# Key-value sums on full-height tiles, values split around a query pass, output transposes behind one wait

## The chip, the cores and the metric

The kernel runs on one core of one Trainium2 chip. The metric is device time in microseconds (us), taken as the median of several executions. A profile is one further execution, recorded by the hardware profiler. TensorE, the matrix engine, is called PE, its weight loads PEld; VectorE is DVE, ScalarE is ACT, GpSimd is POOL, and SP is the engine that issues most DMAs.

## What is computed

Input x has 2048 rows of 448. It is normalised row by row (xn), and two branches are added to it: linear attention with 16 heads of width 28 and a learned feature map, and a feed-forward branch of width 1792.

```python
q, k, v = split_heads(xn @ wqkv)                 # 16 heads, Dh = 28
pq, pk  = q @ w_phi, k @ w_phi                   # per head
phi_q = concat(softmax(pq), softmax(-pq))        # 56 features
phi_k = concat(softmax(pk), softmax(-pk))
kv  = einsum("sf,sd->fd", phi_k, v);  z = phi_k.sum(s)     # per head, over all rows
o   = (phi_q @ kv) / (phi_q @ z + 1e-6)
out = x + concat_heads(o) @ wo + silu(xn @ w1) @ w2
```

The sums kv and z run over all rows, so no query row can be finished before the last key row is in.

## The kernel before

**Tiles.** The rows are worked on as 8 pairs (`NPAIR`) of two tiles of 128 rows (t = 0, 1). All contractions over the 448 features are written for half-height tiles: `mms` issues two matmuls of 64 rows each, one on partitions 0 to 63 (`UP`) and one on 64 to 127 (`LO`), into two banks of PSUM, and PE works on both at once. `contract` makes two passes of this, the second with the halves exchanged; the second pass adds into the banks that the other half wrote, so each of its steps waits (`syncs`) for the last step of the first pass to be complete. With four k-steps in the first pass and three in the second, a pass over 448 columns is 8 or 6 matmuls.

**Stages.** First normalisation and transposes of xn, the folding of w_phi into the key and query weights, and the first layer of the feed-forward branch for pairs 0 to 5 (`ffn1_chunk`). Then the projection stage, one round for each pair p: keys (`k_macro`, name pk_mm, banks 0 and 1), values (v_mm, banks 2 and 3), one group of queries (`q_group`, pq_mm, banks 6 and 7, 512 columns). ACT takes exp of keys (twice 128x896 elements) and of queries (twice 128x1024). DVE copies the values to SBUF (v_ev), sums the keys' exponentials (Sk), takes reciprocals (Rk), and POOL multiplies (phik); for pair 7 this is done tile by tile, with the second tile's phik on DVE. `k_acc(p)` then adds pair p into the sums: for each of 2 tiles, 2 signs and 4 groups of heads one step of four matmuls, 64 rows by 64 columns with 58 columns streamed, two of them into bank 4 (rows 0 to 63) and two into bank 5 (rows 64 to 127). DVE joins the two banks into KVZ under a mask (kvA, then kvz twice). In the last stage, for each pair, `q_products` (U_mm) multiplies queries by KVZ into banks 2 to 5, `q_divide` normalises on DVE (L888 to L901) and adds the two signs on POOL in five pieces (oadd, L920), `o_transpose` turns the result with 14 transposes on PE into banks 6 and 7, from where ACT writes oT (oT_ev), and `out_pair` accumulates 14 matmuls of w2 and 4 of wo for each tile in banks 0 and 1; DVE adds x and SP stores.

**Order.** Nothing is issued in the order in which it is written down. `P.op` records an operation with an estimated duration, its data dependences (`deps`, turned into semaphore waits between engines) and order-only dependences (`odeps`, same engine). `schedule` then makes a static list schedule with these estimates, and each engine runs its list in order. A `prio` of 0 goes before 1 and 2: the feed-forward layer for pairs 6 and 7 has prio 1 and the output tiles prio 2, so they fill PE where the rest is expected to wait. A change of tile shape on PE (`table`) is charged 98 ns in this plan. The projection stage is the exception: its PE order is written out as a chain of order-only dependences,

```python
chain += [k12[0], v12[0], k12[1], v12[1], q12[0], kv, q12[1]]     # L841, kv = k_acc(p - 2)
chain += [k_acc(NPAIR - 2), k_acc(NPAIR - 1)]                     # L842, after the loop
```

with index 0 and 1 for first and second pass. So the key-value sums of pair p - 2 lie between the first and the second query pass of pair p, and for p = 0 and 1 nothing lies there. Prio 1 work can lie between entries of the chain.

**Buffers.** Ek (exponentials of the keys) and vaug (values with a column of ones) have 3 slots (NEK) in one tensor `scr`, first all Ek, then all vaug. `wraw` holds raw query and key weights early and the float32 output of q_divide (`o_both`) late.

## Time and profile before

| what | value |
|---|---|
| median of 3 runs | 165.26 us (164.93 to 165.86) |
| the profiled execution, time and span | 165.84 us, span 164.1 us |
| PE busy | 158.3 us, 96% of the span |
| DVE, ACT, POOL busy | 102.3, 73.8, 54.5 us |
| granted PE clock | 1.00 throughout |
| key-value matmuls, 64x64 tiles, 58 columns (L444) | 512, from 58.2 to 89.6 us |
| output transposes (L457, from 103 us on) | 112, from 103.3 to 140.0 us |

The span is the time from the first to the last instruction of the program in the profile; the execution's own time is 1.74 us longer. Rows of groups give busy time and the mean of one instruction, but matmuls are pipelined: what one costs is read from the distance of starts in the timeline, where a row is a run of like instructions (start, duration with the modelled end of the last, count). The chain of waits is the work that ended last, followed back from the end of the run.

### The profile page before, as it was taken

The page shows a single profiled execution, that of the slowest core. Times are in us where ns is not written, and L with a number is a line of the kernel's source. Part 1 is how long each engine was busy: PE and PEld are TensorE (multiplying, and loading weights), DVE is VectorE, ACT ScalarE, POOL GpSimd, SP SyncE. Part 2 cuts the span into 40 slices and gives each one's busy share as a digit, 9 for nine tenths or more (in the row PEclk, how much of TensorE's full clock was granted, in tenths as well). Part 3 has the DMA queues.
Part 4 walks back from the last instruction along what each step waited for, and adds up shares of the span by engine and source line. Part 5 has one row for each costly group of instructions (what it writes and reads, how often), then busy time and mean ns, then how long its engine had stood idle before and what let it go on. Part 6 is the DMA issues. An engine that isn't in the chain of part 4 may idle for free.

```text
span 164.1 us, 5978 instructions
## 1 busy us (share of the span) xinstructions
PE 158.3 (96%) x2741; PEld 102.7 (63%) x2741; DVE 102.3 (62%) x185; ACT 73.8 (45%) x85; POOL 54.5 (33%) x79
## 2 busy tenths in 40 slices
PE   6999999999999999999999999999999999999994
PEld 4689799999754455545557865555555554455563
DVE  2859878932418887666878788578867865111211
ACT  3542756569688866786667562210220131200000
POOL 7021130110001777755574052553464265000000
PEclk9999999999999999999999999999999999999999
DMA  5974743000003332120000000010101010101011
GB/s 162 311 202 116 203 129 108 0 4 4 4 0 112 116 112 60 46 72 4 4 4 6 0 4 4 0 56 4 50 10 56 0 60 2 56 3 56 0 62 50
DMA packets 8197, 9.24 MB, mean 56 GB/s; under 512 B 1324, under 2 KB 7916, under 8 KB 8172
## 3 DMA queue, kind: packets, MB, share of 16 engines
q1 hardware_dynamic: 7868, 8.62, 17.1%
q8 instruction: 21, 0.34, 0.8%
q10 hardware_dynamic: 304, 0.25, 0.5%
q14 instruction: 4, 0.03, 0.1%
HBM read 7.02 MB, written 1.84 MB: 54 GB/s over the span
## 4 chain that ended last, share of the span: by engine, by line
PE 83%; DVE 7%; DMA 3%; ACT 2%; SPq 2%; issue 1%; DVEq 0%; ACTq 0%
PE psum L444 47%; PE psum L438 33%; PE psum L457 3%; DMA w_sb<-in_B_w_dram 3%; DVE scr L798 2%; SPq L536 2%; DVE wraw L901 1%; DVE Sk L795 1%; ACT oT L463 1%; ACT scr L463 1%; DVE den L892 1%; DVE KVZ L854 1%; DVE kvt L849 0%; DVE R L888 0%; DVE rden L895 0%
## 5 line engine op out<-in xcount | busy, mean ns | idle before, releaser
L444 PE MATMUL psum<-xnT,w_sb 64*128 64x256 bf16 (+1 forms) x938 | 49.4, 252 | 1.0 <-DMA w_sb<-in_B_w_dram 0.6
L438 PE MATMUL psum<-w_sb,hT 128*128 128x448 bf16 (+2 forms) x238 | 47.1, 342 | 0.0
L444 PEld LDWEIGHTS psum<-xnT,w_sb 64*128 64x128 bf16 x938 | 39.2, 94 | 5.4 <-PE psum L444 1.1
L463 ACT ACTIVATE hT<-psum 128x1024 bf16<-128x1024 f32 (+2 forms) x29 | 28.5, 995 | 21.7 <-PE psum L444 21.7
L438 PEld LDWEIGHTS psum<-w_sb,hT 128*128 128x128 bf16 x238 | 22.0, 98 | 18.9 <-issue 0.4
L798 POOL TENSOR_TENSOR scr<-scr,Rk 128x1792 bf16<-128x1792 bf16 (+1 forms) x8 | 24.2, 3021 | 22.8 <-DVE Rk L797 15.3
L920 POOL TENSOR_TENSOR xn_sb<-wraw 128x8 bf16<-128x8 f32 (+4 forms) x40 | 21.3, 564 | 30.1 <-DVE wraw L901 23.8
L941 DVE TENSOR_TENSOR out_sb<-psum,x_sb 128x448 bf16<-128x448 f32 (+2 forms) x17 | 10.1, 595 | 22.1 <-PE psum L438 22.1
L463 ACT ACTIVATE oT<-psum 128x896 bf16<-128x896 bf16 x8 | 7.3, 917 | 33.8 <-PE psum L457 28.3
L463 ACT ACTIVATE EqT<-psum 128x1024 bf16<-128x1024 f32 x16 | 15.5, 1021 | 8.4 <-PE psum L444 8.4
L901 DVE TENSOR_TENSOR wraw<-psum,Gq 128x1792 f32<-128x1792 f32 (+1 forms) x9 | 16.3, 1814 | 1.0 <-DVE Gq L896 0.5
L795 DVE TENSOR_REDUCE Sk<-scr 128x64 f32<-128x1792 bf16 (+1 forms) x9 | 16.2, 1811 | 1.1 <-ACT scr L463 0.5
L467 DVE CAST scr<-psum 128x896 bf16<-128x896 f32 x8 | 8.8, 1094 | 11.7 <-PE psum L444 11.7
L438 PE MATMUL psum<-wo_sb,oT 128*128 128x448 bf16 (+2 forms) x68 | 14.9, 342 | 0.1
L444 PE MATMUL psum<-xnT,wqk_sb 64*128 64x512 bf16 x112 | 14.8, 378 | 0.1
L463 ACT ACTIVATE scr<-psum 128x896 bf16<-128x896 f32 x16 | 13.8, 914 | 1.0
L599 POOL TENSOR_TENSOR rstd<-ve,neghalf 128x2 f32<-128x2 f32 (+1 forms) x8 | 5.3, 660 | 24.2 <-DVE ve L598 24.2
L444 PE MATMUL psum<-wqk_sb,xnT 64*128 64x448 bf16 x112 | 13.2, 349 | 0.0
L444 PE MATMUL psum<-wv_sb,xnT 64*128 64x448 bf16 x112 | 13.2, 349 | 0.0
L590 DVE BATCH_NORM_STATS2 st<-x_sb 128x6 f32<-128x448 bf16 x16 | 9.7, 613 | 3.6 <-DMA x_sb<-in_A_x_dram 3.6
L438 PEld LDWEIGHTS psum<-wo_sb,oT 128*128 128x128 bf16 x68 | 6.4, 98 | 5.9 <-ACT oT L463 0.5
L444 PEld LDWEIGHTS psum<-wqk_sb,xnT 64*128 64x128 bf16 x112 | 5.4, 94 | 5.4 <-ACT scr L463 0.2
(54 smaller groups left out, 120.1 us busy)
## 6 DMA issues: line engine op xcount, KB each, us to landing
out_dram<-out_sb SPq DMA_DIRECT2D x7, 224.0 KB, 2.0
w_sb<-in_B_w_dram SPq DMA_DIRECT2D x3, 448.0 KB, 3.3
x_sb<-in_A_x_dram SPq DMA_DIRECT2D x2, 448.0 KB, 3.4
w_sb<-in_B_w_dram SPq DMA_DIRECT2D x2, 384.0 KB, 4.7
x_sb<-in_A_x_dram SPq DMA_DIRECT2D x3, 224.0 KB, 5.7
wraw<-in_A_wqkv_dram SPq DMA_DIRECT2D x1, 672.0 KB, 4.3
w_sb<-in_B_w_dram SPq DMA_DIRECT2D x1, 576.0 KB, 6.4
wv_sb<-in_A_wqkv_dram SPq DMA_DIRECT2D x1, 336.0 KB, 4.0
```

The lines of the kernel that those rows point to most:

```text
L438: lambda e: e.matmul(dst, lhsT, rhs, start=start, stop=stop, skip_group_check=True),
L444: r = e.matmul(dst, lhsT, rhs, start=start, stop=stop, skip_group_check=True)
L457: out = e.transpose(dst, src, ident[r, 64:128] if r == LO else ident[r, 0:64])
L463: return P.op("act", d_act(_cols(src)), lambda e: e.activation(dst, src, func, scale=scale), reads=[src], writes=[dst], table=table, name= ...
L467: return P.op("dve", dur, lambda e: e.tensor_copy(dst, src), reads=[src], writes=[dst], name=name)
L590: P.op("dve", 600, lambda e: e.bn_stats(st6[:, t, :], x_sb[:, t, :]), reads=[x_sb[:, t, :]], writes=[st6[:, t, :]], name="bnst")
L599: P.op("pool", 580, lambda e: e.tensor_tensor(r2, v2, nh, ALU.pow), reads=[v2, nh], writes=[r2], name="rstd")
L795: P.op("dve", d_dve(896 * n), lambda e, S4=S4, E4=E4: e.tensor_reduce(S4, E4, AXL.X, ALU.add), reads=[E4], writes=[S3], name="Sk")
L798: P.op("dve" if t0 else "pool", d_dve(896) if t0 else d_pool(896 * n, 1.57), lambda e, E4=E4, R4=R4, n=n: e.tensor_tensor(E4, E4, R4[:, :, ...
L901: P.op("dve", d_dve(896 * n), lambda e, dsto=dsto, U=U, G3=G3, n=n: e.tensor_tensor(dsto, U[:, :, :, 0:DH], G3[:, :, :, None].broadcast_to ...
L920: P.op("pool", d_pool(_cols(dst), 2.26), lambda e, dst=dst, a0=a0, a1=a1: e.tensor_tensor(dst, a0, a1, ALU.add), reads=[a0, a1], writes=[d ...
L941: P.op("dve", d_dve(c1 - c0), lambda e: e.tensor_tensor(dst, ob, xs, ALU.add), reads=[ob, xs], writes=[dst], name="out_ev")
```

## The change

It does five things. (1) `k_acc` takes whole 128-row operands: a step is two matmuls of 128 rows by 64 columns instead of four of 64 by 64, and all go to bank 4; kvA and the two kvz become one operation from bank 4 to KVZ. (2) The sums of two pairs lie together between the query passes of p = 3, 5 and 7 (pairs p - 3 and p - 2), where before one pair lay there for p = 2 to 7; a fourth slot for Ek and vaug is taken from wraw, and the slots are laid out one by one. (3) For p = 0, 1, 2, 4, 6, of the three steps of the second value pass the last lies between the two query passes. (4) All sums of pairs 6 and 7 depend on the last phik, and lie together. (5) Every output transpose of a pair depends on the last oadd of that pair. The planned duration of a key-value step goes from 33 to 27 ns.

```diff
@@ -368,18 +368,19 @@
         BD = sb("BD", [128, 5, 56], BF16)
         hT = sb("hT", [128, FT, 2, NPAIR, 128], BF16)
         EqT = sb("EqT", [128, 4, 2, 2, NPAIR * 128], BF16)
-        NEK = 3
+        NEK = 4
+        SLOT = 2 * (EW + H * DV)
         wraw = sb("wraw", [128, 4, 2 * D + 64], BF16)
         o_both = wraw[:].rearrange("p k c -> p (k c)")[:, 0:8 * D].bitcast(F32).rearrange("p (q c) -> p q c", q=4)
-        scr = sb("scr", [128, NEK * 2 * (EW + H * DV)], BF16)
+        scr = sb("scr", [128, 3 * SLOT], BF16)
         wT = scr[:, 0:9 * 512].rearrange("p (a c) -> p a c", a=9)
-        Ek = scr[:, 0:NEK * 2 * EW].rearrange("p (b t c) -> p b t c", b=NEK, t=2)
-        vaug = scr[:, NEK * 2 * EW:NEK * 2 * (EW + H * DV)].rearrange("p (b t h d) -> p b t h d", b=NEK, t=2, h=H)
+        slots = [scr[:, i * SLOT:(i + 1) * SLOT] for i in range(3)] + [wraw[:].rearrange("p k c -> p (k c)")[:, 0:SLOT]]
+        Ek = [a[:, 0:2 * EW].rearrange("p (t c) -> p t c", t=2) for a in slots]
+        vaug = [a[:, 2 * EW:SLOT].rearrange("p (t h d) -> p t h d", t=2, h=H) for a in slots]
         NOB = 3
         o_sum = xn_sb
         oT = sb("oT", [128, NOB, 7, 128], BF16)
         KVZ = sb("KVZ", [128, 2, 4, 2, DZ], BF16)
-        kvt = sb("kvt", [128, 8, 2, DV], F32)
         ident = sb("ident", [128, 128], BF16)
         ones_bf = sb("ones_bf", [128, 128], BF16)
         ones4 = sb("ones4", [128, 4], F32)
@@ -783,13 +784,13 @@
             k12 = proj(p, lambda r, k: wqk_sb[r, k, 1, :, 0:56], 0, "pk_mm")
             kb = psum[:, 0:1024].rearrange("p (t c) -> p t c", t=2)[:, :, 0:D]
             for s in range(2):
-                exp_act(Ek[:, sl, :, s * D:(s + 1) * D], kb, 1.0 if s == 0 else -1.0, "exp_k")
+                exp_act(Ek[sl][:, :, s * D:(s + 1) * D], kb, 1.0 if s == 0 else -1.0, "exp_k")
             v12 = proj(p, lambda r, k: wv_sb[r, k, :], 2, "v_mm")
             vb = psum[:, 1024:2048].rearrange("p (t c) -> p t c", t=2)[:, :, 0:D].rearrange("p t (h d) -> p t h d", h=H)
-            copy_dve(vaug[:, sl, :, :, 0:DH], vb, "v_ev", d_dve(896))
+            copy_dve(vaug[sl][:, :, :, 0:DH], vb, "v_ev", d_dve(896))
             for t0, t1 in ((0, 2),) if p < NPAIR - 1 else ((0, 1), (1, 2)):
                 n = t1 - t0
-                E4 = Ek[:, sl, t0:t1, 0:2 * D].rearrange("p t (h f) -> p t h f", f=DH)
+                E4 = Ek[sl][:, t0:t1, 0:2 * D].rearrange("p t (h f) -> p t h f", f=DH)
                 S3, R3 = Sk[:, sl, 32 * t0:32 * t1], Rk[:, sl, 32 * t0:32 * t1]
                 S4, R4 = (a.rearrange("p (t h) -> p t h", t=n) for a in (S3, R3))
                 P.op("dve", d_dve(896 * n), lambda e, S4=S4, E4=E4: e.tensor_reduce(S4, E4, AXL.X, ALU.add),
@@ -808,14 +809,13 @@
                 for s in range(2):
                     for c in range(4):
                         parts = []
-                        for i, r in enumerate((UP, LO)):
-                            for j in range(2):
-                                hp = 2 * c + j
-                                parts.append((banks[4 + i][64 * j:64 * j + 64, (4 * s + c) * 58:(4 * s + c + 1) * 58],
-                                              Ek[r, sl, t, s * D + hp * 56:s * D + hp * 56 + 64],
-                                              vaug[r, sl, t, 2 * hp:2 * hp + 2, :].rearrange("p h c -> p (h c)"),
-                                              first and s == 0 and c == 0, last))
-                        ops.append(mms(parts, "kv_mm", 33.0, 32))
+                        for j in range(2):
+                            hp = 2 * c + j
+                            parts.append((banks[4][64 * j:64 * j + 64, (4 * s + c) * 58:(4 * s + c + 1) * 58],
+                                          Ek[sl][:, t, s * D + hp * 56:s * D + hp * 56 + 64],
+                                          vaug[sl][:, t, 2 * hp:2 * hp + 2, :].rearrange("p h c -> p (h c)"),
+                                          first and s == 0 and c == 0, last))
+                        ops.append(mms(parts, "kv_mm", 27.0, 32))
             return ops
 
         def q_group(ch, c):
@@ -828,32 +828,34 @@
             return done
 
         for sl in range(NEK):
-            P.op("pool", d_pool(32), lambda e, sl=sl: e.memset(vaug[:, sl, :, :, DH], 1.0),
-                 writes=[vaug[:, sl, :, :, DH]], name="vaug1")
-            P.op("pool", d_pool(16), lambda e, sl=sl: e.memset(Ek[:, sl, :, 2 * D:EW], 0.0),
-                 writes=[Ek[:, sl, :, 2 * D:EW]], name="ekpad")
+            P.op("pool", d_pool(32), lambda e, sl=sl: e.memset(vaug[sl][:, :, :, DH], 1.0),
+                 writes=[vaug[sl][:, :, :, DH]], name="vaug1")
+            P.op("pool", d_pool(16), lambda e, sl=sl: e.memset(Ek[sl][:, :, 2 * D:EW], 0.0),
+                 writes=[Ek[sl][:, :, 2 * D:EW]], name="ekpad")
         P.cur_prio = 0
         chain = []
         for p in range(NPAIR):
             k12, v12 = k_macro(p)
-            kv = k_acc(p - 2) if p > 1 else []
             q12 = q_group(p // 4, p % 4)
-            chain += [k12[0], v12[0], k12[1], v12[1], q12[0], kv, q12[1]]
-        chain += [k_acc(NPAIR - 2), k_acc(NPAIR - 1)]
+            if p > 1 and p % 2:
+                chain += [k12[0], v12[0], k12[1], v12[1], q12[0], k_acc(p - 3), k_acc(p - 2), q12[1]]
+            else:
+                chain += [k12[0], v12[0], k12[1], v12[1][:2], q12[0], v12[1][2:], q12[1]]
+        kv = k_acc(NPAIR - 2) + k_acc(NPAIR - 1)
+        ready = [o.id for o in P.ops if o.name == "phik"][-1]
+        for o in kv:
+            o.deps.add(ready)
+        chain.append(kv)
         chain = [c for c in chain if c]
         for a, c in zip(chain, chain[1:]):
             for o in c:
                 o.odeps.add(a[-1].id)
 
-        bA, bB = (banks[4 + i][:, 0:464].rearrange("p (a h d) -> p a h d", a=8, h=2) for i in range(2))
+        bA = banks[4][:, 0:464].rearrange("p (a h d) -> p a h d", a=8, h=2)
+        dkv = KVZ[:].rearrange("p s c h d -> p (s c) h d")[:, :, :, 0:DV]
         P.op("dve", d_dve(464), lambda e: e.tensor_tensor(
-            kvt[:], bA, mask2[:, None, :, None].broadcast_to([128, 8, 2, DV]), ALU.mult),
-            reads=[bA, mask2[:]], writes=[kvt[:]], name="kvA")
-        for hl in range(2):
-            src, tt, dst = bB[:, :, hl, :], kvt[:, :, hl, :], KVZ[:].rearrange("p s c h d -> p (s c) h d")[:, :, hl, 0:DV]
-            P.op("dve", d_dve(232), lambda e, src=src, tt=tt, dst=dst, hl=hl: e.scalar_tensor_tensor(
-                dst, src, mask2[:, hl:hl + 1], tt, ALU.mult, ALU.add),
-                reads=[src, mask2[:, hl:hl + 1], tt], writes=[dst], name="kvz")
+            dkv, bA, mask2[:, None, :, None].broadcast_to([128, 8, 2, DV]), ALU.mult),
+            reads=[bA, mask2[:]], writes=[dkv], name="kvz")
 
         UB = 2
         U4 = psum[:, UB * 512:UB * 512 + 2048].rearrange("p (q c) -> p q c", q=4)[:, :, 0:480].rearrange("p q (h c) -> p q h c", c=DZ)
@@ -873,6 +875,8 @@
                                           EqT[r, c, s, t, p * 128:(p + 1) * 128],
                                           KVZ[r, s, c, :, :].rearrange("p h d -> p (h d)"), True, True))
                         mms(parts, "U_mm", 31.0)
+
+        oadd_last = {}
 
         def q_divide(p):
             q = p % 2
@@ -920,11 +924,14 @@
                 P.op("pool", d_pool(_cols(dst), 2.26), lambda e, dst=dst, a0=a0, a1=a1: e.tensor_tensor(dst, a0, a1, ALU.add),
                      reads=[a0, a1], writes=[dst], name="oadd")
 
+            oadd_last[p] = P.ops[-1].id
+
         def o_transpose(p):
             ob = o_sum[:, p % NOB, :]
             for j in range(7):
                 trs([(bank16[6 + h][:, 64 * j:64 * j + 64], ob[r, 128 * j:128 * j + 128], r)
                      for h, r in enumerate((UP, LO))], "oT_tr")
+                P.ops[-1].deps.add(oadd_last[p])
             src = psum16[:, 6 * 1024:8 * 1024].rearrange("p (b c) -> p b c", b=2)[:, :, 0:448].rearrange(
                 "p b (j u) -> p b j u", u=64)
             act(oT[:, p % NOB, :, :].rearrange("p j (b u) -> p b j u", b=2), src, ACTF.Identity, "oT_ev")
```

## The prediction

> **What bounds it now.** I read the busy shares first (PE 96% at full granted clock), then the chain of waits by line and in order of time, then PE's timeline stage by stage. The chain as a whole:
>
> ```profile
> PE 83%; DVE 7%; DMA 3%; ACT 2%; SPq 2%; issue 1%; DVEq 0%; ACTq 0%
> ```
>
> PE's own work sets the end, with one interruption of note. In the chain in order of time (start, duration, what) it is this:
>
> ```profile
> 53.98 28.33 PE psum L444 x558
> 82.31 0.02 issue
> 82.33 1.73 ACT scr L463 x2
> 84.07 0.02 issue
> 84.09 2.08 DVE Sk L795 x2
> 86.17 0.48 DVE Rk L797 x2
> 86.65 0.02 issue
> 86.67 2.64 DVE scr L798
> 89.32 0.04 issue
> 89.36 0.66 PE psum L444 x32
> 90.02 0.02 issue
> 90.05 0.65 DVE kvt L849
> 90.70 0.02 issue
> 90.72 0.84 DVE KVZ L854 x2
> ```
>
> Up to 82.3 us every nanosecond that PE is spared is earned. From there the last pair's exponentials, their sums and the second tile's phik (86.67 to 89.31) lead to KVZ at 91.56 and, over the DVE steps of L888 to L901, to the query product at 97.80; PE fills that time with feed-forward matmuls. Behind it PE is packed again to the end: from 140.43 us every output matmul takes 189 ns.
>
> PE's timeline of the projection stage (start, duration, group; duration includes a modelled tail, so I go by starts):
>
> ```profile
> 52.89 1.92 PE L444 MATMUL psum<-xnT,wqk_sb 64*128 64x512 bf16 x14
> 54.64 0.92 PE L444 MATMUL psum<-wqk_sb,xnT 64*128 64x448 bf16 x8
> ...
> 62.37 1.03 PE L444 MATMUL psum<-xnT,wqk_sb 64*128 64x512 bf16 x8
> 63.33 0.89 PE L444 MATMUL psum<-scr 64*64 64x58 bf16 x64
> 64.14 0.82 PE L444 MATMUL psum<-xnT,wqk_sb 64*128 64x512 bf16 x6
> ```
>
> and the output transposes of the last two pairs:
>
> ```profile
> 134.14 0.29 PE L457 MATMUL psum<-ident,xn_sb 64*128 64x64 bf16 x8 [0.23 <-ACT oT L463]
> 134.36 0.36 PE L438 MATMUL psum<-w_sb,hT 128*128 128x448 bf16 x1
> 134.66 0.26 PE L457 MATMUL psum<-ident,xn_sb 64*128 64x64 bf16 x6
> ...
> 138.74 0.26 PE L457 MATMUL psum<-ident,xn_sb 64*128 64x64 bf16 x6
> 138.94 0.36 PE L438 MATMUL psum<-w_sb,hT 128*128 128x448 bf16 x1
> 139.23 0.20 PE L457 MATMUL psum<-ident,xn_sb 64*128 64x64 bf16 x2
> ```
>
> **The empty gap (p = 0, 1).** Both query passes stand in one row of 14 matmuls, 52.89 to 54.64 = 1.75 us; seven steps at 0.216 us (the spacing within a pass) are 1.51. So 0.24 us are lost to the second pass's wait. The value step put there takes 0.19 us (448 columns: 0.76 us for eight matmuls) and is taken out elsewhere. Gain 0.19 x 2 = **0.38 us**, 0.05 of wait staying.
>
> **One visit of key-value sums now.** A round with one lasts 59.72 to 64.80 = 5.08 us; a round without lasts 50.24 to 54.64 = 4.40, less the 0.24 of wait 4.16. So a visit costs 0.92 us: 64 matmuls and two changes of tile shape of about 0.09 each. The visit of p = 7 costs only 0.73 (64 matmuls from 83.65 to 84.29). Single starts in the trace tell why: a step of four stands 31.7 ns behind the one before as long as PE has instructions in hand; in the rounds p = 2 to 6 this ends after ten steps, and then a step takes 59 ns, 14.8 for each matmul and its load. PE is being fed too slowly.
>
> **One visit after.** No row shows a tile of 128 rows by 64 columns. Half the instructions per step: feeding allows 2 x 14.8 = 29.5 ns. From the array's side the nearest rows are pairs of half-height matmuls of like length (transposes, 64 columns: 27.2 ns a pair; U_mm, 60 columns: 28.4) and the present step of 31.7. I take 29 ns, ends 27 and 31.7. Shape changes: U_mm and transposes between output matmuls pay 0.11 going in and 0.12 going out, so 0.21 a visit. 32 steps: 0.93 + 0.21 = **1.14 us** for two pairs.
>
> Up to pair 7's key pass (80.05 us): before 5 x 0.92 = 4.60; after 2 x 1.14 (p = 3, 5) + 3 x 0.05 (waits left at p = 2, 4, 6) = 2.43. Saved 2.17, with the 0.38 above **2.55 us**.
>
> **What the moved step delays.** In even rounds the values are complete 0.86 + 0.19 us later, 3.5 us into the round; v_ev (1.09) then ends at 4.80, and the next value pass over banks 2 and 3 begins at 4.97: covered, by 0.17 less a semaphore's delay. Behind v_ev on DVE stand Sk and Rk; round 6's Rk then ends 3.3 us into round 7, and v_ev(7) and Sk(7) start 0.44 us later than now. Exps of keys end 4.0 us into a round of 4.2, so banks 0 and 1 are free in time. phik, which POOL ends well over 2 us ahead of its visit, loses no cover. The w2 and wo loads hang on exps of even rounds and start sooner. Two more memsets on POOL (0.11 and 0.16 us each) lie in its 11.5 us of idle time before 52.8.
>
> **From round 7 to KVZ.** Work: round 7's visit 1.14 for 0.73 (+0.41); the last two pairs now cost 0.73 + 0.74 without waiting, after 1.14 (-0.33). Together +0.08. The chain: +0.44 (above); behind the last phik stand 32 steps of 29 ns (0.93) instead of 8 (0.25), +0.68; one KVZ operation of 0.64 for 0.65 + 0.84 and a gap, -0.87. So +0.25. Waiting: PE now loses 0.48 between the tiles of pair 7 (64 matmuls take 0.99 us from first to last start, not 0.51), 0.13 before the first U_mm and 0.54 before 97.80. The new wait on the last phik stands in front of 32 steps, and behind it in PE's list lie U_mm and all fillers. The plan gives that phik 1.08 us (`d_dve(896)`), the trace 2.63, so PE should arrive early by over 1 us where it now loses 0.48: I take +0.6 us of waiting. Ends: all three waits gone but for the longer chain (-0.9), and +1.2. Sum of this part **-0.7 us**.
>
> **Transposes in one go.** An interruption costs a change in and out, 0.23 us: (134.66 - 134.36 = 0.30, less 0.19 for the matmul = 0.11) plus 0.12. Pair 6 has one too many, pair 7 two: **+0.69 us**. Their wait for oadd's last piece costs nothing while w2 matmuls lie ahead of them, as they do; without that cover PE would stand up to 2.7 us (five oadd pieces). The wait of 0.4 us for oT before 134.14 might go as well; end +0.4. Pairs 0 to 5 already go 14 at a time.
>
> **Sum.** 2.55 - 0.7 + 0.7 = 2.55 us. The profiled execution's span of 164.1 becomes 161.55, its time of 165.84 would be 163.3; it lies 0.58 above the median. From the median of 165.26: **162.7 us**.
>
> **Rivals.** *(a) Weights are not loaded under running matmuls on full-height tiles: slower.* Today a step has tiles of two row halves, and one half can load while the other runs; afterwards both tiles fill all rows. For it: the two steps at the start of a visit, where no weights lie ready, stand 52 ns apart (83.65 to 83.70), and a 64x64 load takes 107 ns by its row. Against it: 128x128 output matmuls of 128 columns, each with new weights, stand 55.9 ns apart, which leaves no room for a load. Price: load 52 + matmul 29 = 81 ns, 52 more for 4 x 32 steps = 6.7 us: 169.4. It decides from a step of about 56 ns on. The Trainium skill, "TensorE: Matmul & The Clock Gate", Part 3 (The mechanism), says that weight loads overlap running matmuls only where the row group differs, which speaks for this; the 55.9 ns row disagrees. *(b) Loads bind only partly,* a step of about 52 ns as at a visit's start: 23 x 128 = 2.9 us back, 165.6, no change. The same page (LDWEIGHTS) gives columns over 1.2, an estimate of 53 ns for 64 columns; the 31.7 ns step, with a 64-column load on every tile, disagrees. *(c) Waiting behind pair 7 grows to its end,* +1.2 and 0.5 more before U_mm, because PE's list is fixed by durations that are wrong: 1.1 to 1.3 us back, 163.9. For it: the plan's phik; against: three chunks of 28 filler matmuls have free banks there (4.6 us). *(d) Waits fall into place:* -0.9 instead of +0.6, or oT's 0.4 as well: 161.1.
>
> **Chances and range.** Forecast 0.55 (its own range 162.0 to 163.5), (c) 0.16, (d) 0.12, (a) 0.08, (b) 0.09. A measurement here tells 0.5% (0.83 us) from no change, so faster is below 164.4: forecast, (d) and most of (c), 0.82; same 0.09; slower 0.09. Range 161.0 to 164.8: it takes in (c) and (d), whose ends are the bounds of step (27 to 31.7 ns is -0.3 to +0.3) and waiting; (a) and (b) are left out.
>
> **What would show it.** Key-value matmuls: 256, about 15 ns apart throughout, 64 in a row within 1.2 us; three visits in the projection stage. Rounds of about 4.2 and 5.3 us in turn; pair 7's key pass near 77.5 us. KVZ written by one operation near 89.3 us. All output transposes in rows of 14. Wrong if the step stands above 40 ns, if even rounds show PE waiting for v_ev or exps, or if PE waits over 2 us between round 7 and the second pair's U_mm.

## The result and the profile after

| | median of runs | against before, 95% interval | profiled span |
|---|---|---|---|
| before | 165.24 us (164.93 to 165.86) | | 164.1 us |
| after | 163.52 us (163.09 to 164.29) | 0.9869 (0.9837 to 0.9901) | 161.4 us |
| after, measured again | 163.45 us (163.06 to 164.18) | 0.9866 (0.9842 to 0.9889) | 161.3 us |

The change makes the kernel faster by 1.3% (1.0 to 1.6). Forecast were 162.7 us and a range of 161.0 to 164.8. The first ratio is not the quotient of the two medians in the table, which is 0.9896 (1.72 us) and lies inside the same interval. The repeat has 163.45 us against 165.80 for before on its own chip, a quotient of 0.9858.

The 2.7 us between the two profiled spans don't all belong to the change. Ahead of the first key pass of the projection stage the profile of every kernel of this study has the same 1023 matmuls, and yet this pass starts anywhere from 45.25 to 46.73 us. So I compare from that start to the end of the span: 118.27 us before, 115.85 after, 115.86 in the second profile of after. The change is worth **2.42 us** there, and the other 0.33 us of the span lie ahead of it. That measure is used below for all kernels. k7 is the start of pair 7's key pass.

The chain of waits as a whole, in the page of after, shows that PE still sets the end, but DVE has a larger part in it than before:

```profile
PE 78%; DVE 11%; DMA 3%; POOL 2%; issue 2%; SPq 2%; ACT 1%; DVEq 0%; POOLq 0%
```

The same chain in order of time, around the last pairs (start, duration, what):

```profile
77.99 2.02 DVE Sk L796
80.01 0.02 issue
80.03 0.55 DVE Rk L798
...
81.59 1.10 DVE Sk L796
82.69 0.02 issue
82.71 0.35 DVE Rk L798
83.06 0.96 DVE Sk L796
84.02 0.02 issue
84.04 0.36 DVE Rk L798
84.41 0.02 issue
84.43 2.21 DVE wraw L799
86.64 0.14 issue
86.78 5.35 PE psum L445 x156
```

Before, DVE came into it with the Sk of the last pair, 4.04 us after that pair's key pass began. Now it is there from the Sk of pair 6 on (77.99), its steps follow each other without a pause, and PE starts on the last sums only when the last phik (84.43, 2.21 us) has ended.

PE's timeline of after (start, duration with the modelled end, group; count last): an even round, a visit, the last pairs, and the output transposes.

```profile
52.30 1.03 PE L445 MATMUL psum<-xnT,wqk_sb 64*128 64x512 bf16 x8
53.16 0.35 PE L445 MATMUL psum<-wv_sb,xnT 64*128 64x448 bf16 x2
53.39 0.82 PE L445 MATMUL psum<-xnT,wqk_sb 64*128 64x512 bf16 x6
...
60.91 1.03 PE L445 MATMUL psum<-xnT,wqk_sb 64*128 64x512 bf16 x8
61.87 1.20 PE L445 MATMUL psum<-scr 128*64 128x58 bf16 x64
63.00 0.82 PE L445 MATMUL psum<-xnT,wqk_sb 64*128 64x512 bf16 x6
...
82.87 3.33 PE L445 MATMUL psum<-xnT,w_sb 64*128 64x256 bf16 x58
86.78 0.69 PE L445 MATMUL psum<-scr 128*64 128x58 bf16 x32 [0.58 <-DVE wraw L799]
87.28 0.70 PE L445 MATMUL psum<-wraw 128*64 128x58 bf16 x32
...
131.81 0.38 PE L458 MATMUL psum<-ident,xn_sb 64*128 64x64 bf16 x14
...
137.13 0.38 PE L458 MATMUL psum<-ident,xn_sb 64*128 64x64 bf16 x14
```

The moved value step (53.16) stands between the query passes. A visit is one row of 64 tall matmuls. Ahead of the last sums PE has 58 filler matmuls; with 54.5 ns for each, the spacing of such rows, they and a shape change of 0.1 us take 3.27 us of the 3.91, so it stands still for 0.64 us. The last transposes go 14 at a time, and the wait of 0.23 us for oT that stood ahead of pair 6's is gone.

One difference lies at the very end, in the last two stores. SP's timeline of after, then of before:

```profile
158.96 0.33 SPq L951 DMA_DIRECT2D out_dram<-out_sb  x1
159.34 0.43 SPq L951 DMA_DIRECT2D out_dram<-out_sb  x1
```

```profile
161.38 0.33 SPq L944 DMA_DIRECT2D out_dram<-out_sb  x1
162.19 0.33 SPq L944 DMA_DIRECT2D out_dram<-out_sb  x1
```

In the order of after only 3 w2 matmuls stand between the last two pieces of the output, in that of before 14. So the two stores come close together: the last one is issued 0.21 us after DVE has finished its data (159.13), before it was 0.03 us (162.16). From the last wo matmul to the end of the span it takes 2.78 us in after and 2.50 in before. after2, no_merge, no_split, whole6 and short_stream end like after (2.77 to 2.78), the other kernels like before (2.49 to 2.50). Where kernels of these two kinds are compared below, 0.28 us of the difference lie here.

### The profile page after: what moved, and what is told of

Same layout as the page of the kernel before. It is cut to its first block, busy times and chain, and to the rows that moved or that the text cites. A ratio compares the mean times of both kernels' runs of the same rounds, so it can differ in the third digit from the quotient of the medians.

```text
span 161.4 us, 5468 instructions
## 1 busy us (share of the span) xinstructions
PE 155.7 (96%) x2485; PEld 100.7 (62%) x2485; DVE 100.3 (62%) x183; ACT 73.7 (46%) x85; POOL 54.6 (34%) x81
## 4 chain that ended last, share of the span: by engine, by line
PE 78%; DVE 11%; DMA 3%; POOL 2%; issue 2%; SPq 2%; ACT 1%; DVEq 0%; POOLq 0%
PE psum L445 41%; PE psum L439 34%; DVE Sk L796 5%; PE psum L458 3%; DMA w_sb<-in_B_w_dram 3%; POOL scr L799 2%; SPq L537 2%; DVE wraw L799 1%; DVE Rk L798 1%; DVE wraw L905 1%; DVE scr L468 1%; DVE wraw L468 1%; ACT oT L464 1%; DVE den L896 0%; DVE out_sb L948 0%
## 5 line engine op out<-in xcount | busy, mean ns | idle before, releaser
L439 PE MATMUL psum<-w_sb,hT 128*128 128x448 bf16 (+2 forms) x238 | 46.4, 342 | 0.0
L445 PEld LDWEIGHTS psum<-xnT,w_sb 64*128 64x128 bf16 x938 | 38.7, 94 | 5.7 <-PE psum L445 1.3
L464 ACT ACTIVATE hT<-psum 128x1024 bf16<-128x1024 f32 (+2 forms) x29 | 28.4, 994 | 20.8 <-PE psum L445 20.8
L799 POOL TENSOR_TENSOR scr<-scr,Rk 128x1792 bf16<-128x1792 bf16 x6 | 19.3, 3212 | 20.2 <-DVE Rk L798 12.3
L445 PE MATMUL psum<-xnT,wqk_sb 64*128 64x512 bf16 x112 | 14.8, 377 | 0.0
L445 PE MATMUL psum<-wv_sb,xnT 64*128 64x448 bf16 x112 | 14.0, 349 | 0.0
L468 DVE CAST scr<-psum 128x896 bf16<-128x896 f32 x6 | 6.5, 1083 | 11.5 <-PE psum L445 11.5
L796 DVE TENSOR_REDUCE Sk<-scr 128x64 f32<-128x1792 bf16 x6 | 12.1, 2010 | 0.0
L464 ACT ACTIVATE scr<-psum 128x896 bf16<-128x896 f32 x12 | 10.4, 914 | 0.8 <-PE psum L445 0.3
L892 DVE RECIPROCAL R<-psum 128x64 f32<-128x64 f32 (+1 forms) x9 | 4.6, 513 | 7.5 <-PE psum L458 6.1
```

What stands on the lines that cost most here:

```text
L439: lambda e: e.matmul(dst, lhsT, rhs, start=start, stop=stop, skip_group_check=True),
L445: r = e.matmul(dst, lhsT, rhs, start=start, stop=stop, skip_group_check=True)
L464: return P.op("act", d_act(_cols(src)), lambda e: e.activation(dst, src, func, scale=scale), reads=[src], writes=[dst], table=table, name= ...
L468: return P.op("dve", dur, lambda e: e.tensor_copy(dst, src), reads=[src], writes=[dst], name=name)
L796: P.op("dve", d_dve(896 * n), lambda e, S4=S4, E4=E4: e.tensor_reduce(S4, E4, AXL.X, ALU.add), reads=[E4], writes=[S3], name="Sk")
L799: P.op("dve" if t0 else "pool", d_dve(896) if t0 else d_pool(896 * n, 1.57), lambda e, E4=E4, R4=R4, n=n: e.tensor_tensor(E4, E4, R4[:, :, ...
```

## The experiments

In the table, U0 is the start of the first U_mm counted from k7, and the last column is the measure named above. Each ratio is against before, from runs beside it on one chip; the kernels ran on several chips, so medians far apart in the table are best compared by their ratios.

| kernel | k7 less first key pass | U0 | median, us | ratio, 95% | first key pass to end |
|---|---|---|---|---|---|
| before | 34.21 | 11.56 | 165.24 | 1 | 118.27 |
| after | 31.97 | 11.40 | 163.52 | 0.9869 (0.9837 to 0.9901) | 115.85 |
| no_merge | as after | as after | 164.58 | 0.9924 (0.9901 to 0.9947) | 116.86 |
| no_split | 32.80 | 10.76 | 163.36 | 0.9856 (0.9833 to 0.9879) | 116.03 |
| half_tiles | 33.23 | 12.56 | 164.88 | 0.9954 (0.9934 to 0.9974) | 117.35 |
| whole6 | 32.16 | 10.76 | 163.11 | 0.9837 (0.9805 to 0.9869) | 115.39 |
| dve_phik | 31.97 | 12.26 | 162.76 | 0.9810 (0.978 to 0.984) | 115.30 |
| no_ready | as after | 10.47 | 162.84 | 0.9807 (0.9776 to 0.9839) | 115.10 |
| tall_only | 33.24 | 10.57 | 164.22 | 0.9911 (0.9879 to 0.9943) | 116.99 |
| plan_phik | as after | 11.96 | 162.29 | 0.9802 (0.9769 to 0.9836) | 115.00 |
| whole6_dve | as whole6 | 11.96 | 162.92 | 0.9834 (0.9798 to 0.9869) | 115.17 |
| ready7_plan | as after | 11.66 | 162.81 | 0.9835 (0.9797 to 0.9872) | 115.23 |
| short_stream | 34.00 | 12.70 | 167.11 | 1.0093 (1.0058 to 1.0128) | 119.16 |

### after2: the changed kernel once more

No edit. It shows how well one profile repeats.

> The changed kernel unaltered, for a firmer ratio. Its one profile was 2.75 us under the profile of before (163.09 against 165.84), its median only 1.72 under. Theory (the steps add up to 2.4 us from the first key pass on, and 0.3 us of the profiles' difference lies ahead of it, where nothing changed): median near 163.1, ratio 0.984 to 0.988, and from the first key pass to the end of the span 115.9 us. Rival (the change gains only 1.7 us and the profile was a lucky one): that stretch 116.5 us or more in this profile.

Measured: 115.86 us from the first key pass to the end, 0.01 from the first profile; the ratio is as expected, the median of 163.45 is 0.35 above what I had named. So I read differences of some tenths of a microsecond in this measure, with one profile for each of the other kernels; in whole times they can't be read. That other kernels repeat as well as this one was not tried.

### half_tiles: the old tile shape in the new order

The sums lie grouped as in after, with four half-height matmuls to a step, two banks and the three DVE operations that join them.

```diff
-                        for j in range(2):
-                            hp = 2 * c + j
-                            parts.append((banks[4][64 * j:64 * j + 64, ...
-                                          Ek[sl][:, t, s * D + hp * 56:s * D + hp * 56 + 64],
+                        for i, r in enumerate((UP, LO)):
+                            for j in range(2):
+                                hp = 2 * c + j
+                                parts.append((banks[4 + i][64 * j:64 * j + 64, ...
+                                              Ek[sl][r, t, s * D + hp * 56:s * D + hp * 56 + 64],
```

> The changed kernel with key-value sums on 64 by 64 tiles in two banks again, two pairs at a visit as in the change, and three DVE operations to KVZ. Theory (PE is fed too slowly for four matmuls a step): steps of 31.7 ns for about ten steps, then 59 ns; a visit of 1.8 us instead of 1.24, 1.7 us over three visits, and 0.4 plus 0.9 us on the last visit and KVZ, of which waiting may swallow a part: 2 to 3 us slower than the changed kernel, about as slow as before. Rival (it is the grouping in fewer visits that pays, not the tile): visits of 1.2 to 1.3 us and under 1 us slower, all of it after the last visit.

Measured: 1.50 us more than after from the first key pass on. PE's timeline of half_tiles at a visit:

```profile
62.06 1.83 PE L446 MATMUL psum<-scr 64*64 64x58 bf16 x128
63.83 0.82 PE L446 MATMUL psum<-xnT,wqk_sb 64*128 64x512 bf16 x6
```

The same sums take 1.77 us from start to start where after takes 63.00 - 61.87 = 1.13. That is 0.64 us a visit, and it accounts for the 1.26 us by which pair 7's key pass comes later: two visits. Grouping two pairs does not by itself help such matmuls: by single starts the first ten steps of four take 32 ns and the others 59, 14.8 a matmul, as the prediction read it in the visits of before. That PE is short of instructions there is a reading and was not tested; in round 7's visit the steps come back to 33 ns after 18 of them, which it does not explain. The loss is less than the 2 to 3 us expected, because round 7's visit takes 1.41 us instead of 1.8 and the last stores give back 0.28: apart from them it is 1.78 us.

### tall_only: the new tile shape in the old order

From before, with nothing but the tall step and one KVZ operation.

```diff
-                        for i, r in enumerate((UP, LO)):
-                            for j in range(2):
...
+                        for j in range(2):
+                            hp = 2 * c + j
+                            parts.append((banks[4][64 * j:64 * j + 64, (4 * s + c) * 58:(4 * s + c + 1) * 58],
+                                          Ek[:, sl, t, s * D + hp * 56:s * D + hp * 56 + 64],
```

> The kernel before with the full-height tiles and the single KVZ operation alone: one pair at a visit in rounds 2 to 7, three slots, nothing moved. Theory: steps of 32 ns throughout, a visit of 0.73 us instead of 0.92, 0.19 x 5 = 0.95 us to the start of round 7, nothing in round 7, and 0.87 us less from the last phik to U_mm: 1.2 to 1.8 us faster than before. Rival (weights load slower on full-height tiles when a visit is short): visits of 0.9 us, and under 0.9 us faster.

Measured: 118.27 to 116.99, a gain of 1.28 us. A visit of one pair in this kernel's PE timeline:

```profile
57.66 0.69 PE L444 MATMUL psum<-scr 128*64 128x58 bf16 x32
58.29 0.82 PE L444 MATMUL psum<-xnT,wqk_sb 64*128 64x512 bf16 x6
```

Rounds with a visit fall from 5.08 to 4.89 us, five times 0.19, which is the 0.97 us by which k7 moves. The tile shape alone is half of what the whole change brings (1.28 of 2.42). With half_tiles, which loses 1.50 of it, both directions agree: it is the largest part.

### short_stream: half the columns, twice the matmuls

Each tall matmul is split into two of 29 columns, each with its own load of 64 weight columns. Nothing is left out.

```diff
-                        for j in range(2):
-                            hp = 2 * c + j
-                            parts.append((banks[4][64 * j:64 * j + 64, (4 * s + c) * 58:(4 * s + c + 1) * 58],
+                        for h in range(2):
+                            for j in range(2):
+                                hp = 2 * c + j
+                                o = (4 * s + c) * 58 + 29 * h
+                                parts.append((banks[4][64 * j:64 * j + 64, o:o + 29],
```

> The changed kernel with each key-value matmul cut in two of 29 columns, each with its own load of the same 64 columns of weights: twice the matmuls. It asks what sets the 31.9 ns of a step of two full-height matmuls with 58 columns. Loads set it: two matmuls still stand 31.9 ns behind the two before, a visit of 32 steps takes 2.04 us more or less, 4 us slower in all. The columns streamed set it: the distance falls to the feeding floor of 29.5 ns or below it (14.8 a matmul), 3.4 to 3.6 us slower.

Measured, in PE's timeline of short_stream:

```profile
62.31 2.21 PE L445 MATMUL psum<-scr 128*64 128x29 bf16 x128
64.46 0.82 PE L445 MATMUL psum<-xnT,wqk_sb 64*128 64x512 bf16 x6
```

128 matmuls start 16.0 ns apart, 32 ns for a pair of them, just as 64 of twice the columns do in after (1005 ns from first to last start, over 63 intervals: 15.95). So between 29 and 58 the streamed columns do not set the step. From the first key pass on the kernel is 3.31 us slower, not 4: four visits cost 1.02 us more each, and the wait of 0.64 ahead of the last sums is gone. What sets the step stays open. It is not shown to be the load of 64 weight columns: U_mm and the transposes load 128 for each matmul, and their pairs start 30 and 29 ns apart. What all these rows share is one matmul with its load on each tile every 29 to 32 ns, the fed steps of half_tiles included; a fixed price for that fits them as well.

### no_split: the values in one piece again

```diff
-                chain += [k12[0], v12[0], k12[1], v12[1][:2], q12[0], v12[1][2:], q12[1]]
+                chain += [k12[0], v12[0], k12[1], v12[1], q12[0], q12[1]]
```

> The changed kernel with all three steps of the second value pass ahead of the first query pass again, in the rounds 0, 1, 2, 4 and 6. Theory: each of these rounds loses 0.24 us of wait instead of 0.05, so rounds of 4.40 us instead of 4.21 and 0.95 us in all, less 0.1 in round 0 that waits for exps anyway: 0.8 to 1.0 us slower than the changed kernel. Rival (the rounds are bound by the exponentials on ACT at about 4.2 us or by the values' copy): rounds of 4.2 to 4.3 us and under 0.4 us.

Measured: the rounds without a visit last 4.40 instead of 4.21 us, as expected, and k7 comes 0.83 us later; but from k7 to the first U_mm it takes 10.76 instead of 11.40, so 0.64 is given back. From the first key pass to the end 0.18 us are left of the 0.8 to 1.0 expected, and the medians (163.36 and 163.45, same chip) do not differ. The reason lies on DVE and POOL. First POOL in after, then DVE in after:

```profile
80.81 3.21 POOL L799 TENSOR_TENSOR scr<-scr,Rk 128x1792 bf16<-128x1792 bf16 x1 [2.85 <-ACT wraw L464]
83.99 1.70 POOL L799 TENSOR_TENSOR wraw<-wraw,Rk 128x896 bf16<-128x896 bf16 x1
```

```profile
84.43 2.20 DVE L799 TENSOR_TENSOR wraw<-wraw,Rk 128x896 bf16<-128x896 bf16 x1
88.18 0.64 DVE L856 TENSOR_TENSOR KVZ<-psum,mask 128x464 bf16<-128x464 f32 x1 [1.55 <-PE psum L445]
```

and the same two in no_split, POOL and DVE:

```profile
84.03 1.70 POOL L799 TENSOR_TENSOR wraw<-wraw,Rk 128x896 bf16<-128x896 bf16 x1
```

```profile
85.31 1.36 DVE L799 TENSOR_TENSOR wraw<-wraw,Rk 128x896 bf16<-128x896 bf16 x1
```

The last phik on DVE takes 2.20 us in after and 1.36 in no_split, for the same 896 elements. In after POOL is busy with its own phik until 85.69, so 1.26 us of DVE's lie beside it; in no_split 85.73 - 85.31 = 0.42. Both times the duration is 0.94 us and the overlap (alone it is 1.09, as whole6_dve shows below). In no_split k7 comes late by 0.83 us, DVE's last phik with it, and POOL's does not.

### whole6 and dve_phik: two ways out of that overlap

whole6 leaves the values of pair 6 alone in one piece, so that POOL's phik of pair 6 starts sooner. dve_phik leaves the split as it is in after, and puts the first tile's phik of pair 7 on DVE as well.

```diff
# whole6
+                n = 3 if p == 6 else 2
-                chain += [k12[0], v12[0], k12[1], v12[1][:2], q12[0], v12[1][2:], q12[1]]
+                chain += [k12[0], v12[0], k12[1], v12[1][:n], q12[0], v12[1][n:], q12[1]]
# dve_phik
-                P.op("dve" if t0 else "pool", d_dve(896) if t0 else d_pool(896 * n, 1.57), ...
+                P.op("dve" if n == 1 else "pool", d_dve(896) if n == 1 else d_pool(896 * n, 1.57), ...
```

> The changed kernel with the values of round 6 alone whole again, ahead of the query pass; rounds 0, 1, 2 and 4 stay split. Theory (the split of round 6 delays v_ev, Sk, Rk and so POOL's phik of pair 6; POOL's phik of pair 7's first tile then runs beside DVE's phik of the second and stretches it from 0.94 to 2.20 us): round 6 takes 4.40 us instead of 4.21, DVE's phik 1.3 to 1.4 us, PE waits less than 0.1 us in front of the last key-value visit, and the first U_mm stands 10.8 us after round 7's start instead of 11.4; 0.45 us faster than the changed kernel, about 163.0. Rival (the last phik is set by the exponentials of pair 7 and not by POOL): DVE's phik stays over 2 us, U_mm at 11.4 us, and the kernel is 0.2 us slower.

> The changed kernel with both phik of pair 7 on DVE, none on POOL. Theory (DVE's phik is stretched by exactly the time that POOL's runs beside it): two phik of 0.94 us each, the last one ends 8.8 us after round 7's start instead of 9.2, and the first U_mm stands 0.3 to 0.4 us earlier. Rival (2.2 to 2.6 us is what this operation costs on this tile): two of over 2 us, the last phik 2 us later and the kernel over 1 us slower.

Measured: whole6 gains 0.46 us over after, as expected; its last phik takes 1.36 us and U0 comes at 10.76. PE's list behind k7 is that of after, and from k7 to the end it takes 83.24 us instead of 83.88: that is the wait of 0.64. dve_phik missed its expectation for the chain. Its two tiles on DVE:

```profile
83.13 1.88 DVE L799 TENSOR_TENSOR wraw<-wraw,Rk 128x896 bf16<-128x896 bf16 x1
...
86.43 1.09 DVE L799 TENSOR_TENSOR wraw<-wraw,Rk 128x896 bf16<-128x896 bf16 x1
```

The second has POOL to itself and takes 1.09; but the first lies beside POOL's phik of pair 6 until 84.06 (0.93 us) and takes 1.88, and in DVE's order it stands ahead of the second tile's sums, so the last phik ends later and U0 moves back by 0.86 us. And yet the kernel is 0.55 us faster than after, 0.28 of it by the last stores. The length of the chain to KVZ, which I had taken for the thing to shorten, can't be what counts here. PE had 80 filler matmuls ahead of the last sums instead of 58 (the plan now has both phik on DVE, one after the other, and expects these sums later), and its wait there fell from 0.64 to 0.30 us by the same count.

### plan_phik: only the planned duration

The work and the dependences of after, with one number of the plan changed from 1.08 to 2.2 us.

```diff
-                P.op("dve" if t0 else "pool", d_dve(896) if t0 else d_pool(896 * n, 1.57), ...
+                P.op("dve" if t0 else "pool", 2200 if t0 else d_pool(896 * n, 1.57), ...
```

> The changed kernel with one number of the plan altered: the last phik is planned at 2200 ns instead of 1084 (it took 2.20 us); no operation changes, only the order on PE, which puts 80 filler matmuls instead of 58 ahead of the last key-value visit. Theory (what the change loses behind round 7 is PE waiting at that visit because the plan's phik is too short): the 0.64 us of waiting there go to zero although KVZ comes 0.5 us later, and the kernel is 0.7 to 1.0 us faster than the changed kernel, about 162.5. Rival (the chain from the last phik over KVZ sets the end): as much slower as KVZ is later, 0.3 to 0.6 us.

Measured: 0.85 us less than after from the first key pass on, 162.29 us, 0.9802 (0.9769 to 0.9836). That is the lowest time of the study; its interval ends just below those of after (from 0.9837 and from 0.9842) and overlaps those of dve_phik and no_ready. PE's timeline of plan_phik:

```profile
82.92 4.53 PE L445 MATMUL psum<-xnT,w_sb 64*128 64x256 bf16 x80
87.38 0.69 PE L445 MATMUL psum<-scr 128*64 128x58 bf16 x32
87.91 0.67 PE L445 MATMUL psum<-wraw 128*64 128x58 bf16 x32
```

80 fillers run up to the last sums, and the wait in front of them is gone, although U0 comes 0.56 us *later* than in after. Fillers that are issued here need not be issued later. Of the 0.85 us, 0.64 are this wait and 0.28 the last stores, which the new order happens to set apart again; other waits and changes of shape cancel to within 0.1. What costs is PE's standing still, not the length of the chain, as long as there are fillers.

### no_ready, ready7_plan, whole6_dve: the wait on the last phik

no_ready drops the dependence of pair 6's and 7's sums on the last phik; ready7_plan keeps it for pair 7 alone, with the plan's 2.2 us; whole6_dve joins whole6 and dve_phik.

```diff
# no_ready
-        for o in kv:
-            o.deps.add(ready)
# ready7_plan, with the edit of plan_phik
-        for o in kv:
+        for o in kv[len(kv) // 2:]:
             o.deps.add(ready)
```

> The changed kernel without the dependence of the sums of pairs 6 and 7 on the last phik; the plan then puts them down in three visits (32, 16 and 16 steps' matmuls of 32, 16, 16). Theory: two more visits cost 2 x 0.22 us of shape changes, but only 8 steps (0.26 us) instead of 32 (1.0) stand behind the last phik, so KVZ comes up to 0.7 us earlier while PE has 0.4 us more to do: within 0.4 us of the changed kernel either way. Rival (the wait on the last phik is what the change loses at its end): over 0.5 us faster.

> The changed kernel with the last phik planned at 2200 ns, and the dependence on it kept for the sums of pair 7 alone, so that pair 6 has a visit of its own, earlier. Theory: one more visit costs 0.22 us, 16 steps (0.5 us) less stand behind the last phik; PE is busy either way, so 0.1 to 0.4 us slower than with the altered plan alone. Rival (KVZ sooner is worth its time): 0.3 us or more faster than that.

> The changed kernel with the values of round 6 whole and both phik of pair 7 on DVE. Theory: POOL's phik of pair 6 is over before DVE's first phik begins or nearly so, which then takes about 1.1 us instead of 1.88; the last phik ends 9.2 us after round 7's start instead of 10.0, and PE, with 80 fillers ahead of the last visit, no longer waits 0.3 us there; round 6 costs 0.19 more: 0.1 us faster than with DVE's phik alone, about 162.65. Rival (POOL does not stretch it): 1.88 us again and 0.2 us slower.

Measured: no_ready brings U0 0.93 us forward and the end 0.75 us, past the 0.5 that its rival had named; without the 0.28 of the last stores it is 0.47. So the common wait is no help while the plan behind it is wrong. With the plan mended it does no harm: ready7_plan is 0.23 us slower than plan_phik by the profile; by their ratios (0.9835 and 0.9802, overlapping intervals) this is not settled. whole6_dve takes both phik of pair 7 out of POOL's way:

```profile
84.51 1.09 DVE L799 TENSOR_TENSOR wraw<-wraw,Rk 128x896 bf16<-128x896 bf16 x1
...
87.02 1.09 DVE L799 TENSOR_TENSOR wraw<-wraw,Rk 128x896 bf16<-128x896 bf16 x1
```

Both take 1.09 us; the first lies beside POOL for 0.08 us only. The time is that of dve_phik (0.13 us less by the profile, ratios of 0.9834 and 0.9810 with overlapping intervals).

### no_merge: the transposes without their common wait

```diff
-                P.ops[-1].deps.add(oadd_last[p])
```

> The changed kernel without the wait of the output transposes on the last oadd, so that they are cut up again (pair 6 in 2 runs, pair 7 in 4). Theory: each cut costs a change of tile shape in and out, 0.23 us; four cuts, 0.9 us slower than the changed kernel, about 164.0 to 164.4. Rival (PE only waits there for other engines, so the cuts are covered): under 0.3 us slower.

Measured: 1.01 us more than after, all of it behind the first wo matmul (60.00 for 58.99 us to the end). PE's timeline of no_merge where pair 7's transposes go:

```profile
136.47 0.26 PE L458 MATMUL psum<-ident,xn_sb 64*128 64x64 bf16 x6
136.66 0.36 PE L439 MATMUL psum<-w_sb,hT 128*128 128x448 bf16 x1
136.96 0.20 PE L458 MATMUL psum<-ident,xn_sb 64*128 64x64 bf16 x2
...
137.77 0.23 PE L458 MATMUL psum<-ident,xn_sb 64*128 64x64 bf16 x4
...
138.23 0.20 PE L458 MATMUL psum<-ident,xn_sb 64*128 64x64 bf16 x2
```

Without the wait, pair 7's 14 transposes fall into four pieces with w2 matmuls between them, and each piece pays a change of shape in and out. By distances of starts a cut costs 0.10 us in and as much out; four cuts, one of them in pair 6, are 0.77, and PE waits 0.2 us more. One profile and the ratios (0.9924 against 0.9866, so 0.96 us) say the same.

## Why the prediction was right, and where its steps were off

The forecast of 2.55 us stands against 2.42 from the first key pass to the end, and against 2.2 us from the ratio of 0.9869 (1.6 to 2.7). The mechanism was that of the forecast; the median came out 0.8 us above 162.7, inside the range, but at the upper end of the forecast's own 162.0 to 163.5 and nearer to rival (c)'s 163.9. The signs named ahead were there: pair 7's key pass at 77.47 us (77.5 forecast), rounds of 4.21 and 5.39 in turn (4.2 and 5.3), KVZ by one operation (at 88.18, forecast near 89.3), transposes in rows of 14. Up to round 7 it gained 0.31 us less than forecast, behind it 0.18 more; that these nearly cancel is luck. Step by step:

**The empty gap, p = 0, 1 (+0.38 us): right.** Rounds without a visit fall from 4.40 to 4.21 us, 0.19 each. Round 0 shows 4.32, since its exps start late (at 48.05, behind a table load on ACT of 1.28 us) and the next key pass waits for them.

**One visit after (1.14 us): mis-sized by 0.10.** The step of 29 ns measured 31.9, the upper end of 27 to 31.7. I had weighed pairs of half-height matmuls (27.2 and 28.4 ns) higher than the present step of 31.7. Those two figures were read too low: from the start of one pair to that of the next it is 29 ns for transposes and 30 for U_mm, and 27.2 and 28.4 are a row's length divided by half a pair too many. The present step was the nearer row; why, stays open (short_stream). The changes of shape, 0.11 and 0.12, were added up to 0.21, and 0.21 is what they came to. A visit costs 1.24 us (a round of 5.39 or 5.40 less the 4.16 of its other work).

**"Saved ... 2.55 us" up to round 7: measured 34.21 - 31.97 = 2.24 us.** Two visits of 0.10 more are 0.2 of the 0.31 missing, round 0 the other 0.11.

**Rivals (a) and (b), loads not hidden: both fall.** The step of 31.9 ns is far below the 52 and 56 from which they decide. The Trainium skill, "TensorE: Matmul & The Clock Gate", has in Part 3 (The mechanism) that loads overlap running matmuls only if the row group differs; the same section says that loads into a background weight buffer are pulled ahead too. Its section on LDWEIGHTS gives an estimate of 53 ns for 64 columns. These tall tiles share all rows and their steps of two stand 31.9 ns apart with a load on each; the measurement decides against both rivals for this shape, and does not show how the loads are hidden.

**"phik, which POOL ends well over 2 us ahead of its visit, loses no cover": wrong, and this step failed.** It looks at PE's visit only. POOL has to come to pair 7's first tile next, and DVE's phik of the second tile runs beside it. The delay of Sk(7) that I did price at 0.44 us measured only 0.08 (it starts 4.12 instead of 4.04 us into the round). But the moved step delays v_ev, Sk and Rk of pair 6, hence POOL's phik of it (80.81 to 84.02), hence POOL's of pair 7 (to 85.69), and DVE pays 2.20 us for what takes 1.09 alone, 1.26 of it beside POOL. The profile of before had already shown the symptom: 2.64 us for an operation planned at 1.08. Without the split the wait of 0.64 us is gone, as no_split shows, so **the split is worth next to nothing in this kernel**. What it is worth with the plan mended, no run shows.

**From round 7 to KVZ (-0.7 us): its sum came near, by luck, its parts did not.** The end moved by 0.18 us in all behind round 7 (118.27 - 34.21 = 84.06; 115.85 - 31.97 = 83.88). The transposes gained 0.77 of it (next item), and 0.20 came because the last fillers no longer lie on both sides of a w2 matmul (99.01 us in before). So about 0.8 were lost. PE waits 0.64 ahead of the last sums, 0.10, 0.09 and 0.74 ahead of U_mm and 0.24 later, 1.81 us instead of 0.48 + 0.24 + 0.15 + 0.64 = 1.51: 0.30 more, where I took 0.6. (Between fillers and U_mm there is no change of shape to take off, as I did for my 0.13 and 0.54: the four fillers at 91.85 in after take 0.21 us to the next U_mm.) Work grew by 0.28 instead of 0.08: round 7's visit 1.24 for 0.73, and the last two pairs 1.24 for 1.47. And 0.28 us lie in the last two stores, for which the forecast had no term. My reason for the wait, that the plan gives this phik half its time, is shown by plan_phik: with that one number changed the wait is gone, and whole6 takes it away by a shorter phik.

**Transposes in one go (+0.69 us): right.** Three cuts are gone, at 0.19 us each 0.58 (I took 0.23). The wait for oT that I had put at the end of the range (+0.4) went too: 0.29 us by the distance of starts, while 0.10 of another wait came in behind pair 6's transposes. Together 0.77. no_merge's 1.01 is not the same sum: it puts four cuts in.

**Rivals (c) and (d)** priced waiting at +1.2 and -0.9. Measured +0.30: neither. The cause that (c) names, a list fixed by durations that are wrong, is there. A part of what (d) had in view is to be had, as plan_phik shows, but by the plan and not by luck.

## What to carry to other kernels

In a static schedule the planned durations are part of the kernel: an operation that takes twice its plan leaves the busiest engine standing, and setting one number right brought more here (0.85 us, 0.57 of it apart from the last stores) than moving a value step (0.2). When a step is moved, follow what it delays not only to its own consumer but to the next thing that the consumer's engine does, and ask what runs beside that. When tiles are reshaped, count how many matmuls each step issues, not only the columns: here 29 and 58 streamed columns took the same time.

## What the hardware showed that I had not expected

**DVE gives way to POOL almost in full.** A DVE product of 896 columns with two operands in SBUF takes 1.09 us alone. Beside a POOL product it takes 0.94 us and the time of the overlap, so an overlap costs its own length less 0.15. Four overlaps fit to 0.03 us: 1.69 us gave 2.63 (before), 1.26 gave 2.20 (after), 0.93 gave 1.88 (dve_phik), 0.42 gave 1.36 (no_split, whole6). POOL's rows don't change (3.21 and 1.70 us throughout). POOL and DVE in before:

```profile
86.66 1.70 POOL L798 TENSOR_TENSOR scr<-scr,Rk 128x896 bf16<-128x896 bf16 x1 [1.63 <-DVE Rk L797]
```

```profile
86.67 2.63 DVE L798 TENSOR_TENSOR scr<-scr,Rk 128x896 bf16<-128x896 bf16 x1
```

It is the same for a much smaller operation, Gq in plan_phik, on DVE and then on POOL:

```profile
91.81 0.19 DVE L900 TENSOR_TENSOR Gq<-R,rden 128x32 f32<-128x32 f32 x1
...
93.39 1.06 DVE L900 TENSOR_TENSOR Gq<-R,rden 128x32 f32<-128x32 f32 x1
```

```profile
93.27 1.13 POOL L924 TENSOR_TENSOR xn_sb<-wraw 128x448 bf16<-128x448 f32 x1 [7.54 <-DVE wraw L905]
```

32 columns take 0.19 us alone and 1.06 beside POOL's oadd, until that ends. Sk, a sum with one input, keeps its 2.02 us beside POOL's phik. The Trainium skill, "SBUF — State Buffer", section "Who interferes with whom", says that a DVE instruction with two inputs in SBUF contends with a GpSimd instruction that reads SBUF and that a sum by `tensor_reduce` never does; the trace agrees, with 2.20 for 1.09 us and 2.02 unchanged. whole6_dve shows what such a pair costs when it is not set side by side: 1.09 us.

**The start of the run scatters.** The first key pass starts between 45.25 and 46.73 us with the same matmuls ahead of it. The sum of PE's longer waits ahead of it goes from 1.79 to 2.79 us, though not in step with the start in every run; what lies behind this was not tried. Six executions of after2 alone have spans of 161.3 to 162.4 us. It is as large as most effects of this study, and the reason to compare from a mark in the trace.
